# Gates of two blocks for two token groups by Strassen's algorithm, with their input sums and the sums for y moved

## Chip, core and metric

One NeuronCore of a Trainium2 chip. The metric is the device time of one execution in microseconds: the median of three runs, beside the range they cover. PE is the matrix engine, DVE, ACT and POOL (GpSimd) the three others that compute, SP issues most DMAs; POOL issues the accumulating ones.

## What is computed

Banded attention, then two gated feed-forward stages on the 1536 x 512 matrix that it gives, all in float32 with weights stored as float64 words:

```python
scores = scale * q @ k.T + bias + band mask           # 8 global keys, 96 local ones
x = softmax(scores) @ v                               # (2, 8, 768, 64) -> 1536 tokens x 512
a = x @ w1                                            # 512 x 1024
b = x @ w2
h = a * b @ w3                                        # 1024 x 1024
x = h @ w_out                                         # 1024 x 512
out = ((x @ w_a) * (x @ w_b)) @ w_out2                # 512 x 1536, 1536 x 512
```

## The kernel before

Every float32 product is made of three matmuls on split operands (upper part times lower part both ways, and upper times upper), so a matrix is held as a pair hi, lo. The upper part is an ACT copy, the lower part a DVE subtraction (`split`, L742 to L745).

The 1536 tokens are three groups of `TG` = 512. The first feed-forward stage has 8 blocks f of 128 columns of w1 and w2. A **gate** (f, group) makes x @ w1 and x @ w2 for a block and a group: 2 weights x 4 chunks of the 512 inputs x 3 = 24 matmuls of 128x512 (`gate`, L680 to L682); ACT copies the second bank with a sign (L688), and DVE multiplies (L689). A **fold** (f) multiplies w3 of the block with w_out in advance (24 matmuls, `fold`, L244 to L246; ACT stores the result in `wq`, L253). When all gates and folds are there, **y** is the product of `wq` with the gates by a seven-product scheme (`y_product`, 336 matmuls at L942); after it come `products` (1008 matmuls on `ab_band`, again seven products per block) and `output` (`o_band`).

What runs when is written out: `self.order` in `feed_start` lists the gates and folds. Before, it is blocks 0 to 3 group by group, gates of block 4, folds 0 and 1, gates of block 5, folds 2 to 7, gates of blocks 6 and 7, then y. Each engine executes its instructions in the order of the program; `moe` walks the list, and between small steps (`yield`) `feed` emits the next stage of weight conversion: ACT L90, L91, DVE L95, L99, L103, ACT L116, DVE L120 for each piece of weights, loaded by SP into a `raw` buffer. At most six pieces wait.

The operands of y are sums of the gates and of quarters of `wq`. `y_steps` makes them: accumulating DMAs on POOL's queue (L810) write sums in place or into the two buffers `kq01` (free after the attention), and `left` and `right` split them (ACT L822 and L744, DVE L823 and L745). `moe` takes one step behind each gate of blocks 6 and 7, `y_product` the others. The first two raw weights of the second stage (`wab_load`, L747) are loaded and joined in the same steps.

A PSUM bank comes from a pool of eight (`bank`). A matmul that starts a new result in a bank waits until the last reader of that bank is done.

## Time and profile before

| | us |
|---|---|
| median of three runs | 599.81 (599.22 to 599.85) |
| the profiled run | 600.89 |
| its span, first to last instruction | 599.1 |
| PE busy | 584.1 (97%) |
| DVE busy | 442.7 (74%) |
| ACT busy | 366.4 (61%) |
| POOL busy | 168.0 (28%) |

The profile is of one execution, whose own time stands beside its span: what lies around the span is 1.8 us. A busy PE here is a row of overlapping matmuls: each is shown with its whole length, longer than the distance to the next one. "Idle before" is the time in which an engine had nothing to run, with what released it. The gates of block 6 begin at 233.90 us and y at 266.5 us.

### The profile page before, as it was taken

To read this page: it belongs to the slowest core of one execution; us is meant where nothing else is said; L and a number is where in the kernel's file an instruction comes from. 1 tells how busy PE (TensorE), PEld (TensorE's weight loads), DVE (VectorE), ACT (ScalarE), POOL (GpSimd) and SP (SyncE) were. 2 spreads that over 40 slices of the span, in tenths; PEclk is the share of its full clock that TensorE was granted. 3 is DMA by queue.
4 is the path that set the end of the run, shared out by engine and by line. 5 is a ranking of instruction groups with operands and counts; after the bars stand their busy time and mean duration, and the time that the engine had idled before them with its cause. 6 is when DMAs were issued, how large, how long until landed. Compare 5 with 4: busy or idle time off the path is not lost.

```text
span 599.1 us, 10254 instructions
## 1 busy us (share of the span) xinstructions
PE 584.1 (97%) x3632; PEld 509.0 (85%) x3632; DVE 442.7 (74%) x942; ACT 366.4 (61%) x802; POOL 168.0 (28%) x226
## 2 busy tenths in 40 slices
PE   6999999999999999999999999999999999999996
PEld 4678997888888888888899888888888888889996
DVE  5897889539967483649999777777777789984781
ACT  5998889847746473648764544444444465895830
POOL 5653765600000000421612022222222221555500
PEclk9999999999999999999999999999999999999999
DMA  8999683326424332796724112122220248999931
GB/s 228 274 248 236 164 222 106 112 70 212 141 71 141 109 102 70 136 231 126 109 33 139 33 50 79 55 70 71 71 71 2 71 133 220 234 146 193 197 95 57
DMA packets 31821, 76.78 MB, mean 128 GB/s; under 512 B 3601, under 2 KB 11281, under 8 KB 31761
## 3 DMA queue, kind: packets, MB, share of 16 engines
q1 hardware_dynamic: 20560, 57.42, 32.4%
q0 software_dynamic: 10624, 17.83, 18.0%
q10 hardware_dynamic: 576, 0.79, 0.5%
q8 instruction: 30, 0.49, 0.4%
q14 instruction: 31, 0.25, 0.1%
HBM read 55.05 MB, written 3.15 MB: 97 GB/s over the span
## 4 chain that ended last, share of the span: by engine, by line
PE 85%; DMA 9%; DVE 2%; SPq 1%; issue 1%; ACT 0%; POOL 0%; DVEq 0%
PE ab_band L942 29%; PE o_band L942 16%; PE y_band L942 10%; PE ab_band L680 6%; PE ab_band L681 6%; PE ab_band L682 6%; DMA kd_band<-in_kq_dram 3%; PE wfp_band L244 2%; PE wfp_band L246 2%; PE wfp_band L245 2%; DMA v_band<-in_v_dram 2%; PE pv_band L527 2%; DMA kq_band<-in_kq_dram 2%; PE pt_band L491 1%; DMA raw_band<-in_moe_w_dram 1%; DMA qd_band<-in_kq_dram 1%
## 5 line engine op out<-in xcount | busy, mean ns | idle before, releaser
L942 PE MATMUL ab_band<-y_band,ws_band 128*128 128x512 f32 (+1 forms) x576 | 110.1, 337 | 0.0
L942 PEld LDWEIGHTS ab_band<-y_band,ws_band 128*128 128x128 f32 x576 | 91.0, 190 | 12.0
L680 PE MATMUL ab_band<-xh_band,w_band 128*128 128x512 f32 (+1 forms) x216 | 81.8, 379 | 0.0
L682 PE MATMUL ab_band<-xh_band,w_band 128*128 128x512 f32 (+1 forms) x216 | 79.0, 366 | 0.0
L681 PE MATMUL ab_band<-xl_band,w_band 128*128 128x512 f32 (+1 forms) x216 | 79.0, 366 | 0.0
L480 POOL TENSOR_SCALAR s_band<-s_band,z_band 128x256 f32<-128x256 f32 (+1 forms) x96 | 58.3, 622 | 38.8 <-DVE z_band L476 17.8
L942 PE MATMUL o_band<-wo_band,gs_band 128*128 128x256 f32 (+1 forms) x360 | 59.1, 326 | 0.0
L942 PE MATMUL y_band<-gs_band,wf_band 128*128 128x512 f32 (+1 forms) x336 | 58.4, 336 | 0.0
L942 PEld LDWEIGHTS o_band<-wo_band,gs_band 128*128 128x128 f32 x360 | 53.0, 190 | 5.9
L942 PEld LDWEIGHTS y_band<-gs_band,wf_band 128*128 128x128 f32 x336 | 51.8, 190 | 6.6
L942 PE MATMUL ab_band<-y_band,wa_band 128*128 128x512 f32 (+1 forms) x288 | 56.4, 338 | 0.0
L91 ACT ACTIVATE raw_band<-raw_band 128x512 int32<-128x512 uint32 x76 | 51.2, 673 | 0.0
L942 PEld LDWEIGHTS ab_band<-y_band,wa_band 128*128 128x128 f32 x288 | 46.0, 190 | 6.1
L689 DVE TENSOR_TENSOR g_band<-ab_band,b_band 128x512 f32<-128x512 f32 (+1 forms) x27 | 16.9, 628 | 45.2 <-ACT b_band L688 45.2
L463 ACT ACTIVATE s_band<-s_band,m_band 128x256 f32<-128x256 f32 (+1 forms) x96 | 46.7, 493 | 3.2 <-DVE m_band L445 3.2
L680 PEld LDWEIGHTS ab_band<-xh_band,w_band 128*128 128x128 f32 x216 | 40.7, 188 | 7.6 <-issue 1.2
L682 PEld LDWEIGHTS ab_band<-xh_band,w_band 128*128 128x128 f32 x216 | 40.6, 188 | 6.7
L681 PEld LDWEIGHTS ab_band<-xl_band,w_band 128*128 128x128 f32 x216 | 40.7, 189 | 6.1
L1144 ACT COPY p_band<-ab_band 128x512 f32<-128x512 f32 (+1 forms) x48 | 22.0, 481 | 33.4 <-PE ab_band L942 33.2
L810 POOL DMA_DIRECT2D wq_band<-wq_band x4 | 4.6, 1157 | 124.7 <-DVE wf_band L823 123.4
L1145 DVE TENSOR_TENSOR u_band<-ab_band,u_band 128x512 f32<-128x512 f32 (+1 forms) x24 | 13.3, 554 | 33.1 <-PE ab_band L942 32.7
L445 DVE CUSTOM_DVE_ANT_0 s_band<-sp_band,bias_band 128x256 f32<-128x256 f32 (+1 forms) x96 | 37.1, 389 | 0.5 <-ACT bias_band L310 0.4
(160 smaller groups left out, 1258.1 us busy)
## 6 DMA issues: line engine op xcount, KB each, us to landing
raw_band<-in_moe_w_dram SPq DMA_DIRECT2D x31, 512.0 KB, 4.6
raw_band<-in_moe_w_out_dram SPq DMA_DIRECT2D x20, 512.0 KB, 4.4
raw_band<-in_moe_w_b_dram SPq DMA_DIRECT2D x12, 512.0 KB, 3.5
raw_band<-in_moe_w_a_dram SPq DMA_DIRECT2D x12, 512.0 KB, 4.3
ga_band<-ga_band POOLq DMA_DIRECT2D x24, 256.0 KB, 6.7
v_band<-in_v_dram SPq DMA_DIRECT2D x12, 256.0 KB, 8.3
kd_band<-in_kq_dram SPq DMA_DIRECT2D x12, 256.0 KB, 7.8
qd_band<-in_kq_dram SPq DMA_DIRECT2D x12, 256.0 KB, 8.3
```

The lines of the kernel that those rows point to most:

```text
L91: nc.scalar.activation(out=low, in_=low.bitcast(U32), func=AF.Copy, scale=2.0**-29)
L244: nc.tensor.matmul(acc, w[:, 1, k % 4, :], o[:, 0, 0, :], start=(k == 0), stop=False)
L445: nc.vector.tensor_tensor_reduce(out=s[:, j, lo:], in0=sp[:, j, lo:], in1=bias[:, 2 * c + j, :], scale=-self.scale, scalar=FLT_MAX, op0=AL ...
L463: nc.scalar.activation(out=s[:, j, lo:], in_=s[:, j, lo:], func=AF.Exp, bias=m[:, j : j + 1], scale=-1.0, accum_out=z[:, j : j + 1],)
L480: nc.gpsimd.tensor_scalar(out=s[:, j, lo:], in0=s[:, j, lo:], scalar1=z[:, j : j + 1], scalar2=1.0, op0=ALU.mult, op1=ALU.mult)
L680: nc.tensor.matmul(p, wl, xh, start=(c == 0), stop=False)
L681: nc.tensor.matmul(p, wh, xl, start=False, stop=False)
L682: nc.tensor.matmul(p, wh, xh, start=False, stop=(c == self.C - 1))
L689: nc.vector.tensor_tensor(out=out[:, at], in0=ps[0], in1=b, op=ALU.mult)
L942: self.nc.tensor.matmul(bank, wt, xt, start=start and i == n == 0, stop=stop and n == 2 and i == len(terms) - 1, skip_group_check=more,)
L1144: copy = lambda out: nc.scalar.copy(out=out, in_=bank)
L1145: plus = lambda t: nc.vector.tensor_tensor(out=t, in0=bank, in1=t, op=ALU.add)
```

## The change

Gates of blocks 5 and 6 for groups 0 and 1 are made together, as a product of a 2 x 2 matrix of weight quarters (w1 and w2, each cut into two halves of the inputs) with a 2 x 2 matrix of x (two groups, two halves of the inputs). The function `pair` makes seven products of 6 matmuls (2 chunks x 3) where there were eight of 6, in the order 1, 7, 6, 4, 5, 2, 3. Three banks serve a block: the results of products 1, 6, 5 and 3 add up in one of them, and what stands there in between is copied by ACT (behind 1, 7 and 6), added by DVE (behind 4, 5 and 2) or multiplied by DVE (behind 2 and 3).

It needs sums of x and of weights. `x_sums` makes four sums of x in the stretch of the gates of group 2 and block 4 and in the folds, by ACT copies, three POOL additions of 128x1024 (into the second `kq01` buffer) and nine accumulating DMAs on POOL; `x_parts` splits them in fold 7 and in the third gate of block 6. `w_sums` makes the weight sums with four POOL subtractions of 128x256 for each block, and two splits. For these blocks the conversion keeps the joined weights (`g`) and stores them with the opposite sign.

In the order of the program the two pairs stand behind all folds and the third gate of block 6; block 5's gates of groups 0 and 1 have left their place ahead of the folds, so folds 2 to 7 come 48 matmuls sooner. Block 7's gates of groups 0 and 1 are made by `two_gates`, weight by weight; its raw weights are loaded into the two `kq01` buffers when the splits of the sums have read them. The first weights of the second stage are loaded in folds 6 and 7. The steps of `y_steps` are cut smaller and put in another order; eleven of them now lie before y: at three products of the pairs and at eight of the places that `ready` numbers in block 7's gates. In fold, gate and y the matmuls are the same.

PE, the stretch behind the last fold. Before, it is the gate of block 6 for group 0: twelve matmuls of the first weight into one bank, then twelve of the second into the next:

```order
L680 MATMUL ab_band_2967<-xh_band_462,w_band_2851 128x512
L681 MATMUL ab_band_2967<-xl_band_463,w_band_2851 128x512
L682 MATMUL ab_band_2967<-xh_band_462,w_band_2851 128x512
L680 MATMUL ab_band_2980<-xh_band_460,w_band_2864 128x512
L681 MATMUL ab_band_2980<-xl_band_461,w_band_2864 128x512
L682 MATMUL ab_band_2980<-xh_band_460,w_band_2864 128x512
```

Now, in pair 5, six matmuls of product 1 end, product 7 follows in a second bank (`th` are the split sums of x, `ws` those of the weights), and product 6 goes into the first bank again:

```order
L1172 MATMUL ab_band_2987<-xh_band_460,w_band_2397 128x512
L1172 MATMUL ab_band_3000<-th_band_2946,ws_band_2904 128x512
L1172 MATMUL ab_band_3000<-th_band_2947,ws_band_2904 128x512
L1172 MATMUL ab_band_3000<-th_band_2946,ws_band_2904 128x512 x2
L1172 MATMUL ab_band_3000<-th_band_2947,ws_band_2904 128x512
L1172 MATMUL ab_band_3000<-th_band_2946,ws_band_2904 128x512
L1172 MATMUL ab_band_2987<-th_band_2962,ws_band_2904 128x512
L1172 MATMUL ab_band_2987<-th_band_2963,ws_band_2904 128x512
```

The bank `ab_band_2987` is taken up again one product after the one that filled it ended.

ACT in the same stretch. Before, between the first gate of block 6 and the third it copies one bank for each gate (`b_band`), with splits for y and the joining of the second stage's first weights between them:

```order
L688 ACTIVATE b_band_2993<-ab_band_2980 128x512
L822 ACTIVATE wf_band_2996<-wq_band_2530 128x1024
L744 CAST gs_band_3001<-g_band_688 128x1024
L688 ACTIVATE b_band_3037<-ab_band_3024 128x512
L744 CAST gs_band_3040<-g_band_925 128x1024
L865 COPY kq_63<-g_band_2424 128x1024
L822 ACTIVATE wf_band_3047<-wq_band_2530 128x1024
L90 ACTIVATE gb_band_3051<-raw_band_3006 128x512
```

Now the copies of the pairs (`p_band`) stand between the split of the weight sums, the conversion of block 7's first raw weights out of `kq_63`, and the first splits for y:

```order
L804 COPY p_band_2994<-ab_band_2987 128x512
L770 CAST ws_band_2996<-sf_band_2921 128x512
L804 COPY p_band_3007<-ab_band_3000 128x512
L804 COPY p_band_3016<-ab_band_2987 128x512
L770 CAST ws_band_3018<-sf_band_2921 128x512
L92 ACTIVATE g_band_3029<-kq_63 128x512
L93 ACTIVATE kq_63<-kq_63 128x512
L118 CAST w_band_3028<-g_band_3029 128x512
L1061 ACTIVATE wf_band_3059<-wq_band_2549 128x1024
L804 COPY p_band_3072<-ab_band_3065 128x512
L804 COPY p_band_3081<-ab_band_3074 128x512
L984 CAST gs_band_3083<-g_band_688 128x1024
```

The conversion of `kq_63` stands ahead of block 6's first copy, `p_band_3072`.

POOL, the accumulating DMAs for y. Before, the sum of `g_band_925` (gates of group 0, blocks 2 and 3) is made early, and the one that adds it into `kq_64` six places later:

```order
L810 DMA wq_band_2530<-wq_band_2531 128x1024
L810 DMA g_band_688<-g_band_1691 128x1024
L810 DMA g_band_925<-g_band_2053 128x1024
L810 DMA wq_band_2531<-wq_band_2839 128x1024
L810 DMA kq_63<-g_band_688 128x1024
L810 DMA g_band_1691<-g_band_2424 128x1024
L810 DMA wq_band_2530<-wq_band_2839 128x1024
L810 DMA g_band_2373<-kq_63 128x1024
L810 DMA kq_64<-g_band_925 128x1024
```

Now, with nothing between them:

```order
L1050 DMA wq_band_2549<-wq_band_2550 128x1024
L1050 DMA g_band_688<-g_band_1691 128x1024
L1050 DMA wq_band_2550<-wq_band_2800 128x1024
L1050 DMA kq_63<-g_band_688 128x1024
L1050 DMA g_band_1691<-g_band_2440 128x1024
L1050 DMA wq_band_2549<-wq_band_2800 128x1024
L1050 DMA g_band_925<-g_band_2053 128x1024
L1050 DMA kq_64<-g_band_925 128x1024
L1050 DMA g_band_2053<-g_band_3138 128x1024
L1050 DMA g_band_2389<-kq_63 128x1024
```

The DMA into `kq_64` now stands directly behind the one that makes its source, `g_band_925`.

The diff, cut to what the change rests on:

```diff
-        self.order += gates(4) + folds(0, 2) + gates(5) + folds(2, 5) + folds(5, nf)
-        for f in range(6, nf):
-            self.order += gates(f)
+        self.order += gates(4) + folds(0, 2) + gates(5)[2:] + folds(2, nf) + gates(6)[2:]
+        self.order += [("pair", f, 0, whole) for f in self.paired]
+        for f in range(7, nf):
+            self.order += [("two", f, 0, whole), gates(f)[2]]
...
+        self.limit = self.load_limit = len(self.pieces) - 2 * (nf - 1 - self.paired[-1])
...
+            j = self.n_loaded - len(self.pieces)
+            if j >= -2:
+                raw = self.kq01[j].rearrange("p a b c -> p (a b c)").rearrange("p (x y) -> p x y", x=shape[1]).bitcast(I32)
+            else:
+                raw = self.unit("raw", shape, I32)
...
+                if key[0] == "w12" and key[1] in self.paired:
+                    g = self.half("g", [P, a, b])
+                    self.kept.setdefault(key[1], []).append(g)
+                    stages = self.convert(t[:, 0], t[:, 1], raw, g, -1.0)
...
+    def x_sums(self):
+        nc = self.nc
+        add = lambda out, a: nc.gpsimd.dma_start(out, f32(a) if a.dtype == F32R else a, accum_op=ALU.add)
+        (h11, l11), (h21, l21) = self.x[0]
+        (h12, l12), (h22, l22) = self.x[1]
+        t3, t1 = (t.rearrange("p a b c -> p a (b c)") for t in self.kq01)
+        self.sums_x = {3: t3, 1: t1}
+        plus = lambda out, x, y: nc.gpsimd.tensor_tensor(
+            out=out.rearrange("p a b -> p (a b)"), in0=x, in1=y, op=ALU.add
+        )
+        flat = lambda t: f32(t).rearrange("p a b -> p (a b)")
+        nc.scalar.copy(out=t3, in_=f32(h22))
+        yield
+        add(t3, l22)
+        yield
+        t2 = self.sums_x[2] = self.unit("t2", [P, 2, TG])
+        nc.scalar.copy(out=t2, in_=f32(h11))
+        yield
+        plus(t1, flat(h12), flat(l12))
+        add(t3, h12)
+        yield
+        plus(t1, t1.rearrange("p a b -> p (a b)"), flat(h11))
+        add(t2, l11)
+        yield
+        t4 = self.sums_x[4] = [self.half("t4", [P, TG]) for _ in range(2)]
+        for c in range(2):
+            nc.scalar.copy(out=t4[c], in_=f32(h21[:, c]))
+        yield
+        plus(t1, t1.rearrange("p a b -> p (a b)"), flat(l11))
+        add(t3, l12)
+        yield
+        for c in range(2):
+            add(t4[c], l21[:, c])
+        yield
+        yield
+        yield
+        add(t2, t3)
+        yield
+        yield
+        yield
+        yield
+        for c in range(2):
+            add(t4[c], t2[:, c])
+        yield
+    def x_parts(self):
+        self.xt = {}
+        for k in (3, 4, 2, 1):
+            t = self.sums_x.pop(k)
+            hi, lo = ((self.unit if k == 3 else self.late)("th", [P, 2, TG], F32R) for _ in range(2))
+            parts = [(t, slice(None))] if k != 4 else [(t[c], c) for c in range(2)]
+            for src, at in parts:
+                self.nc.scalar.copy(out=hi[:, at], in_=src)
+            yield
+            for src, at in parts:
+                self.nc.vector.tensor_tensor(out=lo[:, at], in0=src, in1=f32(hi[:, at]), op=ALU.subtract)
+            self.xt[k] = hi, lo
+            yield
+    def w_sums(self, f):
+        a, b = self.kept.pop(f)
+        low, high = slice(0, 2), slice(2, 4)
+        if f == self.paired[-1]:
+            st = self.unit("sf", [P, 2, 2, 2, P])
+            s, t = st[:, 0], st[:, 1]
+        else:
+            s, t = (self.half("sf", [P, 2, 2, P]) for _ in range(2))
+        sub = lambda out, x, y: self.nc.gpsimd.tensor_tensor(out=out, in0=x, in1=y, op=ALU.subtract)
+        sub(t[:, 0], b[:, low], b[:, high])
+        sub(s[:, 1], a[:, low], t[:, 0])
+        sub(s[:, 0], b[:, low], a[:, low])
+        sub(t[:, 1], a[:, high], s[:, 1])
+        yield
+        self.ws[f] = []
+        for g in (s, t):
+            w = self.unit("ws", [P, 2, 2, 2, P], F32R)
+            self.ws[f].append(w)
+            self.nc.scalar.copy(out=w[:, 0], in_=g)
+            yield
+            self.nc.vector.tensor_tensor(out=w[:, 1], in0=g, in1=f32(w[:, 0]), op=ALU.subtract)
+            yield
+    def late_parts(self):
+        x, (v, w), o = self.x_parts(), self.w_parts, iter(())
+        for part in (v, v, w, v, v, x, x, x, x, x, x, x, x, o, o, o, w, o, w, o, w, o, w, o):
+            next(part, None)
+            yield
+    def pair(self, f, w, gu, extra):
+        nc = self.nc
+        a, b = w
+        s, t = self.ws.pop(f)
+        part = lambda t, *at: [(t[(slice(None), 0, *at, c)], t[(slice(None), 1, *at, c)]) for c in range(2)]
+        whole = lambda t, cs: [(t[:, 0, c], t[:, 1, c]) for c in cs]
+        left = {
+            1: whole(a, (0, 1)), 2: whole(a, (2, 3)), 4: whole(b, (2, 3)),
+            7: part(s, 0), 6: part(s, 1), 5: part(t, 0), 3: part(t, 1),
+        }
+        right = {1: self.x[0][0], 2: self.x[0][1], 3: self.x[1][1], 7: 3, 6: 2, 4: 4, 5: 1}
+        banks, kept = {}, {}
+        for k in (1, 7, 6, 4, 5, 2, 3):
+            if k in (1, 7, 2):
+                bank = banks[k] = self.bank("ab")
+            bank = banks[{4: 7, 7: 7, 2: 2}.get(k, 1)]
+            hi, lo = self.xt[right[k]] if k > 3 else right[k]
+            self.multiply(bank, left[k], [(hi[:, c], lo[:, c]) for c in range(2)], k in (1, 7, 2), True, k in (6, 4, 5, 3))
+            if k in (1, 7, 6):
+                kept[k] = self.half("p", [P, TG])
+                nc.scalar.copy(out=kept[k], in_=bank)
+            elif k == 3:
+                if f // 2 not in gu[1]:
+                    gu[1][f // 2] = self.late("g1", [P, 2, TG])
+                nc.vector.tensor_tensor(out=gu[1][f // 2][:, f % 2], in0=bank, in1=kept[7], op=ALU.mult)
+            else:
+                t = kept[{4: 6, 5: 7, 2: 1}[k]]
+                nc.vector.tensor_tensor(out=t, in0=bank, in1=t, op=ALU.add)
+                if k == 2:
+                    if f // 2 not in gu[0]:
+                        gu[0][f // 2] = self.late("g1", [P, 2, TG])
+                    nc.vector.scalar_tensor_tensor(
+                        out=gu[0][f // 2][:, f % 2], in0=t, scalar=-1.0, in1=kept[6], op0=ALU.mult, op1=ALU.mult
+                    )
+            for _ in range(2):
+                next(extra, None)
+            yield 1.4
...
+    def two_gates(self, pair, xs, outs, signs):
+        nc = self.nc
+        banks = []
+        for n, w in enumerate(pair):
+            for m, x in enumerate(xs):
+                p = self.bank("ab")
+                banks.append(p)
+                for c in range(self.C):
+                    wh, wl, (xh, xl) = w[:, 0, c, :], w[:, 1, c, :], x(c)
+                    nc.tensor.matmul(p, wl, xh, start=(c == 0), stop=False)
+                    nc.tensor.matmul(p, wh, xl, start=False, stop=False)
+                    nc.tensor.matmul(p, wh, xh, start=False, stop=(c == self.C - 1))
+                    if c == 1:
+                        yield 1.3
+                if n:
+                    b = self.half("b", [P, TG])
+                    nc.scalar.mul(b, p, signs[m])
+                    nc.vector.tensor_tensor(out=outs[m], in0=banks[m], in1=b, op=ALU.mult)
+                yield 1.3
...
+        def ready(i):
+            if i in (0, 1, 2, 3, 5, 8, 9, 11):
+                next(prepare)
+            if i == 4:
+                self.wab_load(1)
+                self.joins[1] = self.wab_join(1)
+            if i > 5:
+                for _ in range(2):
+                    next(self.joins[1], None)
...
+            if what == "pair":
+                if prepare is None:
+                    prepare = self.y_steps(gu)
+                for k, turn in enumerate(self.pair(f, pairs.pop(f), gu, extra)):
+                    if (f, k) in ((5, 6), (6, 1), (6, 4)):
+                        next(prepare)
+                    if (f, k) == (self.paired[0], 0):
+                        self.load_limit += 2
+                        self.feed_load(self.load_limit)
+                    if (f, k) in ((self.paired[0], 3), (self.paired[1], 3)):
+                        self.limit += 1
+                    yield turn
+                continue
...
-        left(1, a11, self.late)
+        left(1, a11)
         add(a11, a21)
+        yield
         right(0, 1, 0, b11[0])
         add(b11[0], b12[0])
-        weights(0, 0)
+        add(a21, a22)
+        yield
+        nc.scalar.copy(out=t2[0], in_=b22[0])
+        add(t2[0], b11[0])
+        add(b12[0], b22[0])
+        yield
+        left(7, a11, self.late)
+        add(a11, a22)
         yield
         right(0, 1, 1, b11[1])
         add(b11[1], b12[1])
-        nc.scalar.copy(out=t2[0], in_=b22[0])
-        add(a21, a22)
-        left(7, a11)
-        weights(0, 4)
-        yield
-        add(t2[0], b11[0])
-        add(b12[0], b22[0])
-        add(a11, a22)
+        yield
         right(0, 2, 0, b21[0])
-        weights(0, 5)
+        yield
+        left(2, a12, self.late, -1.0)
         yield
         b21, b22 = ([gu[t][2 + j] for j in range(2)] for t in range(2))
         c11, c12, c21, c22 = ([gu[2][j + e][:, :, at] for j in range(2)] for e in (0, 2) for at in ends)
-        left(2, a12, self.late, -1.0)
-        right(0, 2, 1, b21[1])
-        add(b21[0], t2[0])
-        yield
         nc.scalar.copy(out=t2[1], in_=b22[1])
         add(t2[1], b11[1])
         add(b12[1], b22[1])
+        yield
+        right(0, 2, 1, b21[1])
+        add(b21[0], t2[0])
+        yield
         left(6, a11, self.unit, -1.0)
         add(a12, a11)
         add(b21[1], t2[1])
...
```

## Rows read from the trace of the kernel before

**Rows 1.** The page: busy time of the engines; TensorE's granted clock in 40 slices.
```profile
PE 584.1 (97%) x3632; PEld 509.0 (85%) x3632; DVE 442.7 (74%) x942; ACT 366.4 (61%) x802; POOL 168.0 (28%) x226
...
PEclk9999999999999999999999999999999999999999
```

**Rows 2.** Waits of PE, whole span: line, releaser: us in total, times, longest.
```profile
PE sp_band L411 <- DMA kq<-in_kq_dram: 5.3, 3, 4.7
...
PE sp_band L428 <- DVE m_band L445: 0.5, 1, 0.5
```

**Rows 3.** The chain of waits in order of time: start us, us, what.
```profile
266.70 58.23 PE y_band L942 x336
324.94 175.88 PE ab_band L942 x1008
```

**Rows 4.** By stretch: busy us of PE, PEld, DVE, ACT, POOL; clock; DMA share; GB/s.
```profile
157.00:165.00 8.00, 8.00 (x37) 6.60 (x37) 7.66 (x14) 5.95 (x15) 0.00 (x0) 1.00 0.39 131
233.90:244.00 10.10, 10.10 (x46) 8.38 (x45) 3.05 (x3) 3.14 (x5) 1.23 (x2) 1.00 0.00 1
244.00:255.00 11.00, 11.00 (x51) 9.09 (x50) 7.60 (x10) 7.21 (x11) 5.01 (x6) 1.00 1.02 190
255.00:266.70 11.70, 11.70 (x53) 9.71 (x52) 4.55 (x6) 4.13 (x5) 2.59 (x3) 1.00 1.06 237
```

**Rows 5.** Timeline of PE: start us, us, engine, line, operation, tiles.
```profile
233.90 0.39 PE L680 MATMUL ab_band<-xh_band,w_band 128*128 128x512 f32 x1
...
239.34 0.39 PE L680 MATMUL ab_band<-xh_band,w_band 128*128 128x512 f32 x1
...
266.54 0.84 PE L942 MATMUL y_band<-gs_band,wf_band 128*128 128x512 f32 x3
```

**Rows 6.** Timeline of ACT, then DVE, behind the first gate of block 6.
```profile
239.54 0.60 ACT L688 ACTIVATE b_band<-ab_band 128x512 f32<-128x512 f32 x1 [4.78 <-PE ab_band L682]
...
240.17 0.69 DVE L689 TENSOR_TENSOR g_band<-ab_band,b_band 128x512 f32<-128x512 f32 x1 [9.62 <-ACT b_band L688]
```

**Rows 7.** Tiles kq, 236 to 300 us: duration ns min/median/max; below, us to landing.
```profile
L744 ACT CAST gs_band<-kq x2: 1054/1057/1060, 270.4 to 273.3; 128x1024 fp32r<-128x1024 f32 x2
L745 DVE TENSOR_TENSOR gs_band<-kq,gs_band x2: 1216/1222/1227, 271.5 to 277.0; 128x1024 fp32r<-128x1024 f32 x2
...
DMA to landing us min/median/max: 7.0/8.4/9.5
```

**Rows 8.** Timeline of DVE, then ACT, 160 to 176 us.
```profile
161.58 0.68 DVE L689 TENSOR_TENSOR g_band<-ab_band,b_band 128x512 f32<-128x512 f32 x1
...
174.95 0.69 DVE L689 TENSOR_TENSOR g_band<-ab_band,b_band 128x512 f32<-128x512 f32 x1 [4.10 <-ACT b_band L688]
...
161.70 0.62 ACT L116 CAST w_band<-g_band 128x512 fp32r<-128x512 f32 x1 [1.26 <-DVE g_band L103]
```

**Rows 9.** Groups of POOL by shape, whole span: count | busy us, mean ns.
```profile
L777 POOL TENSOR_TENSOR sf_band<-ga_band,sf_band 128x256 f32<-128x256 f32 x12 | 13.4, 1114 | 0.9
...
L777 POOL TENSOR_TENSOR sf_band<-ga_band,gb_band 128x256 f32<-128x256 f32 x12 | 9.3, 774 | 48.4 <-DVE ga_band L103 48.4
```

**Rows 10.** Timeline of DVE while POOL adds (128x1024 operations).
```profile
299.99 1.64 DVE L745 TENSOR_TENSOR y_band<-u_band,y_band 128x1024 fp32r<-128x1024 f32 x1
301.56 1.75 DVE L955 TENSOR_TENSOR p_band<-u_band,p_band 128x1024 f32<-128x1024 f32 x1
```

**Rows 11.** Tiles raw_band (raw weights), 130 to 300 us: time to landing.
```profile
DMA to landing us min/median/max: 3.4/4.2/12.3
```

**Rows 12.** Timeline of POOL, ACT and DVE around the sums for y.
```profile
242.67 1.03 POOL L810 DMA_DIRECT2D wq_band<-wq_band  x1 [123.43 <-DVE wf_band L823]
...
266.71 1.06 ACT L822 ACTIVATE wf_band<-wq_band 128x1024 fp32r<-128x1024 f32 x1 [3.00 <-DMA wq_band<-wq_band]
...
277.04 1.22 DVE L745 TENSOR_TENSOR gs_band<-kq,gs_band 128x1024 fp32r<-128x1024 f32 x1
```

**Rows 13.** Tiles wq_band, 236 to 300 us: time to landing of the accumulating DMAs.
```profile
DMA to landing us min/median/max: 4.7/9.1/15.0
```

More of the change, by code (lines that the diff above doesn't have):

```diff
@@ L49, in __init__ @@
         self.pairs_from = 16
+        self.paired = (5, 6)
+        self.kept, self.ws = {}, {}
         self.sums = {}
@@ L723, in moe @@
             }[tg]
-            yield from self.gate(pairs[f], xs(tg), gu[tg][q][:, f % 2], at, signs)
-            if n == last[f]:
+            if f == self.paired[-1]:
+                for _ in sums:
+                    pass
+            for turn in self.gate(pairs[f], xs(tg), gu[tg][q][:, f % 2], at, signs):
+                if tg == 2 and 0 < f < 4 or f == 4 and tg:
+                    next(sums, None)
+                if f == self.paired[-1]:
+                    for _ in range(3):
+                        next(extra, None)
+                if f == nf - 1:
+                    ready(early)
+                    early += 1
+                yield turn
+            if f == self.paired[-1]:
+                for _ in range(3):
+                    next(extra, None)
+            if n == last[f] and f not in self.paired:
                 pairs[f] = None
-            if f >= nf - 2:
-                if prepare is None:
-                    prepare = self.y_steps(gu)
-                next(prepare)
+            if f >= nf - 1:
+                ready(early)
+                early += 1
             yield 1.3 * (at.stop - at.start) / TG
@@ L847, in adds @@
                 add(out[j], a[j])
-        def weights(f, n):
-            if f not in joins:
-                self.wab_load(f)
-                joins[f] = self.wab_join(f)
-            for _ in range(n):
-                next(joins[f], None)
-        joins = {}
-        left(1, a11, self.late)
+        left(1, a11)
         add(a11, a21)
+        yield
         right(0, 1, 0, b11[0])
         add(b11[0], b12[0])
-        weights(0, 0)
+        add(a21, a22)
[6 more added lines that the diff above has]
+        add(a11, a22)
         yield
@@ L881, in y_steps @@
         yield
-        nc.scalar.copy(out=t2[1], in_=b22[1])
-        add(t2[1], b11[1])
-        add(b12[1], b22[1])
         left(6, a11, self.unit, -1.0)
@@ L895, in y_steps @@
         right(0, 6, 1, t2[1])
-        weights(1, 3)
         yield
```

58 lines of the change are left out of this document (47 added, 11 removed).

## Prediction

> **What bounds the kernel now.** I read the page's engine summary first, then the waits of PE, the chain of waits, the table by stretch, and last the single rows around the places that the change touches. The summary has PE busy for 97% of the span, at a granted clock that never falls [rows 1]. All of PE's waits together are about 10 us, all at lines of the attention (the longest group 5.3 us, the shortest 0.5 us) [rows 2]. From the y product on the chain of waits is PE alone, in two unbroken pieces that meet without a gap (266.70 + 58.23 = 324.93 against 324.94) [rows 3]. In the stretches shown, from 157 to 165 and from 233.9 to 266.7 us, PE is busy from end to end, while DVE has 15.2 us of work in the last three, 32.8 us [rows 4]. So here a matmul removed is its time gained, as long as everything that PE needs still comes before PE asks for it.
>
> The pace: the gates of blocks 6 and 7 are 144 matmuls of 128x512; the first starts at 233.90, the first of y at 266.54 [rows 5]. 32.64 / 144 = 0.2267 us each. (The 0.39 us in the rows is one matmul's own length; they overlap.)
>
> **The change, term by term.** The sum is made against the profiled run (600.89 us, span 599.1) and put on the median, 599.81, as a difference.
>
> *Removed.* A block's gates for groups 0 and 1 are 2 groups x 2 weights x 4 chunks x 3 = 48 matmuls; the seven products are 7 x 2 chunks x 3 = 42. Two blocks: 12 fewer, 12 x 0.2267 = **2.72 us**, all on PE's path. Nothing else is taken from or given to PE: folds, y, the later products and the output keep their matmuls.
>
> *Added on ACT and DVE.* With 0.60 us for a 128x512 copy and 0.69 for a DVE operation of that size [rows 6], 1.05 and 1.22 us for 128x1024 [rows 7]: ACT gets 3.3 (copies of x) + 4.35 (upper parts of the x sums) + 2.4 (of the weight sums) + 3.6 (six copies per block) - 2.4 (four evacuations gone) = 11.3 us. DVE gets 5.0 + 2.7 + 10 x 0.69 - 2.8 = 11.8 us. Both have that room under PE, so I take nothing for it, unless one operation is late for its place. There are four such places.
>
> 1. *Hand-offs of the banks inside a block.* A product is 6 x 0.2267 = 1.36 us, and in PE's new order the same bank is written again one product after its result was read: four tight hand-offs per block, eight in all. Before, the first matmul behind a gate starts at 239.34, ACT's copy runs 239.54 to 240.14, DVE's operation takes 0.69 [rows 5, 6]. So a copy is over 0.80 us into the next product and a DVE add 0.20 + 0.69 = 0.89: 0.56 and 0.47 us to spare. In ACT's new order only one of these copies (block 6, third product) has a 1.05 us operation right ahead of it, which itself starts early; it keeps about 0.3. Cost taken: 0; bound: the spare times are used up eight times by a 1.05 us operation, 8 x 0.49 = 3.9.
>
> 2. *The x sums, at 142 to 165 us.* Here DVE is nearly full (7.66 of 8.00 us) [rows 4] and behind PE: it reads the second gate of group 2 only at 161.58 and is done by 162.26 [rows 8], while that bank is wanted again 300 matmuls ahead of 233.90, at 165.9: 3.6 us to spare. New there are four ACT copies and three GpSimd adds of 128x1024. ACT's next conversion step waits for DVE anyway (1.26 us idle before it) [rows 8], so a copy in front delays little. A GpSimd add of 128x256 took 0.77 to 1.11 us on the mean [rows 9], so an estimate for 128x1024 is four times that, 3.1 to 4.5 us; the first falls just ahead of that read. Beside such adds DVE's 1.22 us operations took 1.64 and 1.75 us [rows 10], 34 to 43% longer: over 4.5 us that is at most 1.9 us, less than 3.6. Cost taken: 0. After it, DVE has an idle gap of 4.10 us [rows 8] before the folds.
>
> 3. *The x parts and block 7's weights.* Pair 5 starts at T = 233.90 - 48 x 0.2267 + 24 x 0.2267 = 228.46 (block 5's gates for two groups now lie behind the folds, block 6's third ahead). ACT's splits queue behind the last fold's evacuation at T - 5.4; counting 0.4 to 1.05 us each, then 0.7 to 1.22 on DVE, the parts are there at T - 1.9 (third sum, wanted at T + 1.36), T + 0.6 (second, T + 2.72) and T + 1.8 (first, T + 5.44). Smallest spare time 2.1 us. Block 7's raw weights now go into the buffers that these splits free, and ACT's conversion of them stands in its queue ahead of block 6's first copy, due at T + 12.2. A load landed 3.4 to 12.3 us after issue [rows 11]; from T - 1.9 that is T + 1.5 to T + 10.4, and with 4.5 us of conversion behind it a stall of up to 2.7 us at the far end, none below a landing at T + 7.7. The median, 4.2, gives none: cost 0.
>
> 4. *The y sums.* The accumulating DMAs begin at about T + 12.5 (block 5 ends at T + 9.5; its last DVE operation 0.9, a split of 1.22, an issue on POOL of 1.03 us [rows 12]), and y at T + 156 x 0.2267 = T + 35.4 = 263.8. The tight one is the second sum in the kq buffers, wanted 54 matmuls into y, T + 47.6. Before, its DVE split ended 277.04 + 1.22 = 278.26 for a need at 266.54 + 12.24 = 278.78: already only 0.5 us early [rows 12]. Now its DMA stands on POOL's queue right behind the one whose result it adds, so it is not issued before that one has landed. With 190 to 237 GB/s [rows 4], 512 KB take 2.2 to 2.8 us; seven adds and one or two raw loads make 17.6 to 25.2 us, so T + 30.1 to T + 37.7. The next add lands 7.0 to 9.5 us later [rows 7], and ACT and DVE need 1.05 + 1.22: ready at T + 39.4 to T + 49.5. The middle (T + 44.6) is 3 us early; the far end 1.8 us late. Cost taken: 0, since the medians leave room.
>
> Sum: 600.89 - 2.72 = 598.2 for the profiled run, **597.1** for the median.
>
> **A rule against the trace.** The [rows 10] show a slowing of DVE beside GpSimd, not a stop. The Trainium skill, "SBUF — State Buffer", section "SBUF: two separate sides", says that DVE operations with two SBUF inputs and GpSimd operations share a port pair by an exclusive lock, so that the loser waits for the whole instruction. The trace is short of that: adds of 0.77 to 1.11 us beside them [rows 9] cost an operation 0.42 and 0.53 us. What a full stop would do is rival D.
>
> **The rivals.**
>
> A (forecast): all 2.72 us arrive. 597.1. For it: PE's unbroken chain, and spare times at each place. Chance 0.60.
>
> B: the hand-offs stall PE by 0.2 to 0.4 us each, 8 x 0.2 to 0.4 = 1.6 to 3.2 us: 598.7 to 600.3, mostly no change. It needs ACT or DVE to be busy with something else at the instant a product ends; the order shows that once in eight, and both engines are about half idle there. Chance 0.13.
>
> C (slower): the chained y sum. If the second of the two adds lands as late as the slowest add before (15.0 us [rows 13]; ACT waited 3.00 us for such an add [rows 12]), its split is ready at T + 37.7 + 15.0 + 2.3 = T + 55.0, a stall of 7.3 us: 604.4. It gives a slower kernel once the stall is over 2.72 + 1.2 = 3.9 us, a landing after T + 49.3; between 1.5 and 3.9 us it cancels the gain. For it: ACT is in order, so later copies wait behind this one, and DMA is full there. Against: the 15.0 was the last of a burst, while this one is issued when the burst is nearly through. Chance 0.18, of which 0.13 slower.
>
> D: GpSimd's first 128x1024 add stops DVE for all of it: 161.58 + 4.5 + 0.68 = 166.8, 0.9 us after the bank is wanted; the other adds fall into DVE's slack. 598.0, still faster. Chance 0.05, half of it with a further stall to no change.
>
> E: PE was not the bound and nothing changes, 599.8. Against it stand [rows 2, 3]: 0.02. A further 0.02 is left for a late weight in place 3 that undoes the gain.
>
> **How the numbers follow.** A measurement of this kernel tells 0.2%, 1.2 us, from no change, so faster means below 598.6. Faster: A 0.60 + half of D 0.03 = 0.63. Same: B 0.11, C 0.05, D 0.02, E and the late weight 0.04 = 0.22. Slower: C 0.13, B 0.02 = 0.15. The likeliest is A, 597.1. The range goes from 596.5 (the runs before lie 0.6 us apart) up through B and the mild end of C to 600.8; about 0.15 is left above and 0.05 below.
>
> **What would show it.** Right: 12 matmuls fewer in PE's rows, pairs of 9.5 us each, y starting 2.7 us sooner (263.8) and no PE wait between 130 us and the end of y. Wrong: a wait of PE on the banks or on ACT copies inside the pairs (B), on the split of a kq buffer about 12 us into y (C), on a gate's bank at 163 to 169 us (D), or DVE operations lengthened there by more than half. If the stalls at places 1 to 4 add up to over 1.5 us, the forecast of a measurable gain falls.

## The result, and the profile after

| | us |
|---|---|
| before, median of nine runs | 599.85 (599.22 to 600.65) |
| changed, median of nine runs | 606.59 (600.67 to 607.05) |
| ratio | 1.0098, 95% interval 1.0073 to 1.0124 |
| profiled run of the changed kernel | 606.28, span 604.3 |

The change makes the kernel 1% slower. The forecast was 597.1, with a range that ended at 600.8. Eight of the nine runs lie between 605.06 and 607.05; of the ninth, 600.67, there is no trace. The profiled run of the kernel before took 600.89, more than any of its nine, so the two profiles differ by less (5.4 us) than the medians (6.74).

The page of the changed kernel, engine summary and granted clock, against [rows 1]. The 12 matmuls are gone (3632 to 3620), and in one slice the clock falls:

```profile
PE 583.3 (97%) x3620; PEld 507.0 (84%) x3620; DVE 466.0 (77%) x957; ACT 376.1 (62%) x817; POOL 191.6 (32%) x246
...
PEclk9999999999979999999999999999999999999999
```

The waits of PE, against [rows 2]. The attention's are as before. Three are new: one for a DVE operation of a gate, two inside y.

```profile
PE ab_band L830 <- DVE g_band L839: 3.9, 1, 3.9
...
PE y_band L1172 <- ACT u_band L1226: 0.7, 1, 0.7
...
PE y_band L1172 <- ACT p_band L1226: 0.4, 1, 0.4
```

**Where 5.2 us of span came from (604.3 against 599.1).** PE came out of the attention 1.06 us sooner in this execution, and from there to 161.90 us every matmul is ahead by that much. (In the traces of the runs below the same matmuls are 0.02 to 1.63 us ahead, in kernels that are the same up to there or nearly so, so this is not put down to the change.) Fold 0 began at 174.06 us before and begins at 179.96 now, 5.90 us later, so 6.96 us were lost from 161.90 on. y then starts at 269.71 where it was 266.54, so 2.73 us were won back between: the twelve matmuls. y itself lasts 60.16 us where it lasted 58.23: 1.93 lost. 6.96 - 2.73 + 1.93 = 6.16 us lost by the change; less the 1.06 of the attention that is 5.10 of the 5.2.

The pairs are what the forecast said they would be. In the timeline of PE the first matmul of block 5's pair and of block 6's:

```profile
234.35 0.39 PE L1172 MATMUL ab_band<-xh_band,w_band 128*128 128x512 f32 x1
...
243.87 0.39 PE L1172 MATMUL ab_band<-xh_band,w_band 128*128 128x512 f32 x1
```

9.52 us, 42 x 0.2267, with no wait; the second pair takes as long (`two_gates` begins at 253.39). The loss is elsewhere, in two places.

**Place one, 153 to 175 us.** Timeline of PE: the first matmul behind a short hold, the last ahead of the long wait, the first behind it, and the first two that come faster again:

```profile
162.41 0.50 PE L830 MATMUL ab_band<-xh_band,w_band 128*128 128x512 f32 x1
...
165.07 0.39 PE L832 MATMUL ab_band<-xh_band,w_band 128*128 128x512 f32 x1
169.32 0.80 PE L830 MATMUL ab_band<-xh_band,w_band 128*128 128x512 f32 x1 [3.86 <-DVE g_band L839]
...
174.18 0.45 PE L832 MATMUL ab_band<-xh_band,w_band 128*128 128x512 f32 x1
174.48 0.40 PE L830 MATMUL ab_band<-xh_band,w_band 128*128 128x512 f32 x1
```

The matmul at 162.41 needs a bank that ACT copies only at 161.69 to 162.36, late because ACT's conversion step at 158.57 had waited 3.66 us for DVE; by 165.07 PE is 0.44 us behind. From 165.07 to 169.32 PE starts nothing: 4.02 us more than a matmul's distance. The twelve matmuls from 169.32 to 174.48 then take 5.16 us where they took 2.72: 2.44 us. Together 6.90 of the 6.96. The table by stretch shows why the twelve are slow: the columns are as in [rows 4], the clock the one ahead of the DMA share:

```profile
167.00:168.00 1.00, 0.00 (x0) 0.00 (x0) 1.00 (x1) 0.00 (x0) 1.00 (x1) 0.74 1.11 221
...
169.00:174.00 5.00, 4.68 (x11) 3.72 (x12) 4.30 (x8) 4.78 (x11) 2.68 (x3) 0.50 1.03 197
...
175.00:176.00 1.00, 1.00 (x6) 0.83 (x5) 0.86 (x2) 0.41 (x1) 0.00 (x0) 1.00 1.12 193
```

With PE idle, the granted clock goes to 0.50, 1.2 GHz, and comes back to 2.4 GHz only at 174 to 175 us, when PE had been at work again for some five us.

What PE waited for is DVE's evacuation of the second gate of group 2, at 168.59 in place of 161.58 [rows 8]. Timeline of DVE:

```profile
153.65 3.33 DVE L97 TENSOR_SCALAR g_band<-g_band 128x512 int32<-128x512 int32 x1
...
162.01 3.45 DVE L101 SCALAR_TENSOR_TENSOR g_band<-raw_band,g_band 128x512 int32<-128x512 int32 x1
165.60 3.07 DVE L105 CUSTOM_DVE_ANT_0 g_band<-raw_band,g_band 128x1024 uint16<-128x1024 uint16 x1
168.59 0.68 DVE L839 TENSOR_TENSOR g_band<-ab_band,b_band 128x512 f32<-128x512 f32 x1
```

The operation at L97 takes 0.42 us alone (as at 161.55, in the same timeline); here 3.33. L101 and L105 take 0.69 alone; here 3.45 and 3.07. Timeline of POOL at the same time:

```profile
153.97 2.71 POOL L699 TENSOR_TENSOR kq<-xh_band,xl_band 128x1024 f32<-128x1024 f32 x1
...
162.20 2.70 POOL L699 TENSOR_TENSOR kq<-kq,xh_band 128x1024 f32<-128x1024 f32 x1
...
165.15 2.96 POOL L699 TENSOR_TENSOR kq<-kq,xl_band 128x1024 f32<-128x1024 f32 x1
```

Each long DVE operation stands beside one of the three GpSimd additions and ends just behind it: additions end at 156.68, 164.90 and 168.11 (start and length added), the operations at 156.98, 165.46 and 168.67. DVE was not slowed, it stood still until GpSimd had finished. It lost 2.91 + 2.76 + 2.38 = 8.05 us. 3.6 of them were to spare, PE itself came 0.44 late, and the rest, 4.0, is PE's wait.

**Place two, y.** Timeline of PE, the rows of y with a wait (0.44 and 0.71 us):

```profile
314.14 8.89 PE L1172 MATMUL y_band<-gs_band,wf_band 128*128 128x256 f32 x72 [0.44 <-ACT p_band L1226]
323.75 6.28 PE L1172 MATMUL y_band<-gs_band,wf_band 128*128 128x256 f32 x48 [0.71 <-ACT u_band L1226]
```

ACT and DVE have no work for over 5 us in the early part of y, which they then lack later. Timelines of POOL, ACT and DVE there, against [rows 12]:

```profile
258.55 0.86 POOL L1050 DMA_DIRECT2D g_band<-g_band  x1 [0.27 <-DVE gs_band L985]
272.03 0.86 POOL L1050 DMA_DIRECT2D kq<-g_band  x1 [12.62 <-ACT gs_band L984]
...
273.63 1.91 POOL L1050 DMA_DIRECT2D wq_band<-wq_band  x1
```

```profile
276.76 1.05 ACT L984 CAST gs_band<-kq 128x1024 fp32r<-128x1024 f32 x1 [3.35 <-DMA kq<-g_band]
...
285.32 3.05 ACT L984 CAST gs_band<-g_band 128x1024 fp32r<-128x1024 f32 x4 [5.59 <-issue]
```

```profile
279.76 1.23 DVE L985 TENSOR_TENSOR gs_band<-g_band,gs_band 128x1024 fp32r<-128x1024 f32 x1 [0.69 <-ACT gs_band L984]
286.40 2.43 DVE L985 TENSOR_TENSOR gs_band<-g_band,gs_band 128x1024 fp32r<-128x1024 f32 x3 [5.41 <-ACT gs_band L984]
```

The add into `g_band`, issued at 258.55, makes the source of the next DMA on POOL's queue. That one goes out at 272.03, after a wait of 12.62 us, and three more stand behind it. The row names ACT as the releaser; in the program this DMA waits for the landing of the other, which took 12.9 us, to 271.45, the longest of the DMAs that read or write `g_band` there:

```profile
DMA to landing us min/median/max: 4.7/8.7/12.9
```

The last of the three, the sum of two quarters of `wq` (273.63), landed 11.6 us after its issue, at 285.23. ACT's next split starts at 285.32 and DVE's at 286.40, after 5.41 us idle. ACT's row names no releaser ("issue"), but the same row of a run below, the one with the sum by DMA, names this DMA:

```profile
279.20 3.04 ACT L985 CAST gs_band<-g_band 128x1024 fp32r<-128x1024 f32 x4 [5.64 <-DMA wq_band<-wq_band]
```

That split reads gates, not this sum, so by the program it can only be waiting for memory that the DMA still uses; no run tests this. A run without this DMA, below, has no such gap.

The delay lasts to the place where PE feels it: ACT's copy of `p_band`, for which the matmuls at 314.14 wait, starts 44.0 us into y, where it started 41.6 us into y before. PE's two waits are 1.15 of the 1.93 us that y lost.

### The profile page after: what moved, and what is told of

It reads as the page before. It is cut to its first block, busy times and chain, and to the rows that moved or that the text cites. A ratio compares the mean times of both kernels' runs of the same rounds, so it can differ in the third digit from the quotient of the medians.

```text
span 604.3 us, 10314 instructions
## 1 busy us (share of the span) xinstructions
PE 583.3 (97%) x3620; PEld 507.0 (84%) x3620; DVE 466.0 (77%) x957; ACT 376.1 (62%) x817; POOL 191.6 (32%) x246
## 4 chain that ended last, share of the span: by engine, by line
PE 68%; DMA 11%; DVE 11%; issue 4%; ACT 3%; SPq 1%; POOL 1%; DVEq 0%; POOLq 0%; ACTq 0%
PE ab_band L1172 32%; PE o_band L1172 15%; DMA kd_band<-in_kq_dram 3%; PE ab_band L830 3%; DMA v_band<-in_v_dram 2%; PE ab_band L831 2%; PE ab_band L832 2%; PE wfp_band L264 2%; PE wfp_band L263 2%; PE wfp_band L262 2%; DMA g_band<-g_band 2%; DVE gs_band L985 2%; PE pv_band L545 2%; DMA kq_band<-in_kq_dram 2%; PE pt_band L509 2%
## 5 line engine op out<-in xcount | busy, mean ns | idle before, releaser
L498 POOL TENSOR_SCALAR s_band<-s_band,z_band 128x256 f32<-128x256 f32 (+1 forms) x96 | 56.9, 608 | 37.5 <-DVE z_band L494 18.0
L830 PE MATMUL ab_band<-xh_band,w_band 128*128 128x512 f32 (+1 forms) x168 | 64.4, 383 | 4.0 <-DVE g_band L839 3.9
L831 PE MATMUL ab_band<-xl_band,w_band 128*128 128x512 f32 (+1 forms) x168 | 61.3, 365 | 0.0
L832 PE MATMUL ab_band<-xh_band,w_band 128*128 128x512 f32 (+1 forms) x168 | 61.1, 364 | 0.0
L93 ACT ACTIVATE raw_band<-raw_band 128x512 int32<-128x512 uint32 x74 | 49.6, 670 | 0.0
L830 PEld LDWEIGHTS ab_band<-xh_band,w_band 128*128 128x128 f32 x168 | 32.2, 192 | 10.8 <-DVE g_band L839 4.3
L1017 POOL TENSOR_TENSOR sf_band<-gb_band 128x256 f32<-128x256 f32 x12 | 10.3, 862 | 94.2 <-DVE gb_band L105 75.2
L118 ACT CAST w_band<-g_band 128x512 fp32r<-128x512 f32 x36 | 22.5, 624 | 25.9 <-DVE g_band L105 25.7
L832 PEld LDWEIGHTS ab_band<-xh_band,w_band 128*128 128x128 f32 x168 | 32.2, 192 | 5.1
L831 PEld LDWEIGHTS ab_band<-xl_band,w_band 128*128 128x128 f32 x168 | 32.3, 192 | 4.4
```

What stands on the lines that cost most here:

```text
L93: nc.scalar.activation(out=low, in_=low.bitcast(U32), func=AF.Copy, scale=2.0**-29)
L118: nc.scalar.mul(hi, g, sign) if sign < 0 else nc.scalar.copy(out=hi, in_=g)
L498: nc.gpsimd.tensor_scalar(out=s[:, j, lo:], in0=s[:, j, lo:], scalar1=z[:, j : j + 1], scalar2=1.0, op0=ALU.mult, op1=ALU.mult)
L830: nc.tensor.matmul(p, wl, xh, start=(c == 0), stop=False)
L831: nc.tensor.matmul(p, wh, xl, start=False, stop=False)
L832: nc.tensor.matmul(p, wh, xh, start=False, stop=(c == self.C - 1))
```

## Experiments

Theory G: a GpSimd addition holds DVE for as long as it runs; the bank comes late; PE waits and its clock falls. Rival R: the copies and DMAs of the x sums delay the weight conversion. For y, theory Y1: sums that land late hold ACT and DVE; rival Y2: DVE has simply too much to do there.

**Without the three additions.**

```diff
-        plus(t1, flat(h12), flat(l12))
...
-        plus(t1, t1.rearrange("p a b -> p (a b)"), flat(h11))
...
-        plus(t1, t1.rearrange("p a b -> p (a b)"), flat(l11))
```

> The changed kernel without the three GpSimd additions of 128x1024 among the x sums; the fourth x sum then holds what lies in its buffer, so that part of the computation is left out. Theory G (a GpSimd addition holds DVE for the length of the whole instruction, the gate's bank comes late, PE waits and its granted clock falls): PE's 3.9 us wait at 165 to 169 us and the stretch at the lower clock are gone, about 6.7 us less than the changed kernel, 598.3 to 599.5 (the forecast 597.1 and the 1.2 us of waits in y). Rival R (ACT's four copies and the accumulating DMAs of the x sums delay the weight conversion): they are all still there, so 605 to 607.

Measured: 599.26, ratio to before 0.9990 (0.9979 to 1.0001). No wait of PE between the attention and y; in y 0.7 and 0.6 us. R falls: all its copies and DMAs are still there, and in its trace PE loses nothing between the attention and fold 0.

**The same sum by DMA.**

```diff
-        plus(t1, flat(h12), flat(l12))
+        nc.scalar.copy(out=t1, in_=f32(h12))
...
+        add(t1, l12)
...
+        add(t1, h11)
...
+        add(t1, l11)
```

The other two `plus` lines are taken out.

> The changed kernel with the same sum made by one more ACT copy of 128x1024 and three more accumulating DMAs, in place of the three GpSimd additions. Theory G: no long DVE instruction between 150 and 170 us, no PE wait there, 598 to 600. Rival R: more copies and more DMA, so as late as the changed kernel or later, 606 to 609.

Measured: 599.96, ratio 0.9988 (0.9976 to 1.0000). One more ACT copy and three more DMAs of 512 KB cost nothing that shows; the additions on GpSimd did.

**The additions cut into quarters.**

```diff
...
+            for i in range(4):
+                at = slice(i * TG // 2, (i + 1) * TG // 2)
+                nc.gpsimd.tensor_tensor(out=o[:, at], in0=x[:, at], in1=y[:, at], op=ALU.add)
```

> The changed kernel with each of the three GpSimd additions cut into four of 128x256: the same work on GpSimd, some 8.4 us, in 12 instructions. Theory G with a hold for a whole instruction: no DVE instruction is longer than its own time plus about 0.8 us, and DVE and GpSimd take turns, so that DVE loses less in all, 3 to 6 us where it lost 8, and PE waits 0 to 2 us: 598.5 to 603. If the two engines shared the port by bandwidth, DVE would lose the same 8 us and the time stay at 605 to 607.

Measured: 608.69, ratio 1.0140 (1.0122 to 1.0158), slower still; the expectation fails. Timelines of POOL and of DVE:

```profile
154.85 3.13 POOL L703 TENSOR_TENSOR kq<-xh_band,xl_band 128x256 f32<-128x256 f32 x4
...
162.89 3.09 POOL L703 TENSOR_TENSOR kq<-kq,xh_band 128x256 f32<-128x256 f32 x4
```

```profile
154.54 3.73 DVE L97 TENSOR_SCALAR g_band<-g_band 128x512 int32<-128x512 int32 x1
...
162.84 3.93 DVE L97 TENSOR_SCALAR g_band<-g_band 128x512 int32<-128x512 int32 x1
```

POOL's rows hold four additions each (x4). DVE gets no turn between them: one DVE operation of 0.42 us lasts 3.73 us, through all four. So here it counts how long GpSimd adds without a break, not how long one instruction is.

**The additions alone, in the kernel before.**

```diff
+                if tg == 2 and 0 < f < 4:
+                    next(sums, None)
```

`sums` is a generator that makes the three GpSimd additions into a kq buffer, one after the other.

> The kernel before with nothing but the three GpSimd additions put in at the same place of the program (into a kq buffer that is not read before it is written again). Theory G: DVE loses about 8 us at 152 to 168 us, the bank of the second gate of group 2 is some 4 us late, PE's clock falls, 604 to 607. Rival R: three additions on an engine that is idle cost nothing, 599.9.

Measured: 599.84, ratio 0.9997 (0.9987 to 1.0007): no loss, against the expectation. But the additions did not run where they were written. Nothing on POOL's queue held them, and they ran 35 us sooner, under the attention. Timeline of POOL, and the DVE operation that ran beside the second of them:

```profile
118.28 2.39 POOL L698 TENSOR_TENSOR kq<-xh_band,xl_band 128x1024 f32<-128x1024 f32 x1
120.75 2.38 POOL L698 TENSOR_TENSOR kq<-kq,xh_band 128x1024 f32<-128x1024 f32 x1
```

```profile
122.40 0.69 DVE L689 TENSOR_TENSOR g_band<-ab_band,b_band 128x512 f32<-128x512 f32 x1 [3.04 <-ACT b_band L688]
```

Alone an addition takes 2.4 us. And this DVE operation, which reads a PSUM bank and one SBUF tile, has its usual 0.69 us: not every DVE operation is held. (Two subtractions of the attention beside the first addition, and two beside the third, read PSUM and SBUF too; they are not held either: 0.76 us for each two, 0.42 for a single one at 111.99.) The experiment as I meant it needed the copy and the DMAs in front, which hold POOL's queue:

**The additions held back, in the kernel before.**

```diff
+        nc.scalar.copy(out=t3, in_=f32(h22))
...
+        add(t3, l22)
...
+        plus(flat(h12), flat(l12))
+        add(t3, h12)
...
+        plus(out, flat(h11))
...
+        plus(out, flat(l11))
```

> The kernel before with the start of the x sums alone: ACT's copy of 128x1024 into the first kq buffer, the two accumulating DMAs into it, and the three GpSimd additions behind them, which so run at 152 to 168 us as in the changed kernel (nothing reads the sums). Theory G: DVE loses about 8 us there, PE waits 3 to 4.5 us for the bank of a gate of block 4 and then runs some 7 us at the lower clock: 604 to 607. Rival (the pairs or the folds in a new order are what costs): 599.9, as in the run whose three additions had run ahead, under the attention.

Measured: 606.99 (four runs, 603.7 to 608.85), ratio 1.0094 (1.0057 to 1.0131). Nothing else of the change is in this kernel, and it loses 6.5 us. POOL, DVE and PE's wait:

```profile
154.93 2.73 POOL L700 TENSOR_TENSOR kq<-xh_band,xl_band 128x1024 f32<-128x1024 f32 x1
...
160.78 2.69 POOL L700 TENSOR_TENSOR kq<-kq,xh_band 128x1024 f32<-128x1024 f32 x1
```

```profile
154.62 3.33 DVE L95 TENSOR_SCALAR g_band<-g_band 128x512 int32<-128x512 int32 x1
...
160.48 3.56 DVE L99 SCALAR_TENSOR_TENSOR g_band<-raw_band,g_band 128x512 int32<-128x512 int32 x1
164.17 2.61 DVE L103 CUSTOM_DVE_ANT_0 g_band<-raw_band,g_band 128x1024 uint16<-128x1024 uint16 x1
```

```profile
PE ab_band L680 <- ACT b_band L688: 4.8, 1, 4.8
```

The bank that PE waits for is here one that ACT frees (the one that cost the changed kernel 0.44 us): ACT's step ahead of that copy had waited 5.58 us for DVE's held conversion. So the hold reaches PE by either engine.

**The additions later, in the folds.**

```diff
-        plus(t1, flat(h12), flat(l12))
...
         for c in range(2):
             add(t4[c], t2[:, c])
...
+        plus(t1, flat(h12), flat(l12))
...
```

The other two additions move likewise.

> The changed kernel with the three GpSimd additions of 128x1024 put behind the accumulating DMAs of the x sums on POOL's queue, so that they run in the first folds, some 25 us later. Theory G says that a GpSimd addition holds DVE whenever it runs: DVE instructions of about 3 us must appear beside them there too, but no gate waits for a bank behind them, so the 3.9 us wait of PE at 165 us and the lower clock behind it are gone: 598 to 601, near the kernel with DMA additions (599.96). If the loss were the additions themselves and not their place, 605 to 607.

Measured: 600.54, ratio 1.0006 (0.9996 to 1.0015). POOL and DVE:

```profile
181.87 3.04 POOL L699 TENSOR_TENSOR kq<-xh_band,xl_band 128x1024 f32<-128x1024 f32 x1
184.99 2.75 POOL L699 TENSOR_TENSOR kq<-kq,xh_band 128x1024 f32<-128x1024 f32 x1
```

```profile
181.81 3.67 DVE L105 CUSTOM_DVE_ANT_0 g_band<-raw_band,g_band 128x1024 uint16<-128x1024 uint16 x1
185.40 2.63 DVE L97 TENSOR_SCALAR g_band<-g_band 128x512 int32<-128x512 int32 x1
```

DVE is held there nearly as long (3.67, 2.63 and 2.77 us, 7.3 us lost), but PE waits for nothing of it at the time. Later it does, a little: 0.7 us for a copy in a pair and 0.2 for a split of an x sum. The gain is still not there; the waits in y (0.7 and 0.5) are.

**The additions on DVE itself.**

```diff
-        plus = lambda out, x, y: nc.gpsimd.tensor_tensor(
+        plus = lambda out, x, y: nc.vector.tensor_tensor(
```

> The changed kernel with the three additions of 128x1024 on DVE itself. There they take 1.22 us each, 3.7 us in all, less than the 8 us that DVE lost to them on GpSimd, and in DVE's order they stand behind the multiplication that frees the bank. Theory G: no PE wait at 165 us; the waits in y remain: 599 to 600.5. If an addition in this stretch costs the same wherever it runs, 605 to 607.

Measured: 598.78, ratio 0.9982 (0.9971 to 0.9993), 0.2 us below the range expected; of PE's waits in y one is left, 0.7 us. DVE, with the evacuation that PE needs ahead of the first of them:

```profile
160.11 0.68 DVE L839 TENSOR_TENSOR g_band<-ab_band,b_band 128x512 f32<-128x512 f32 x1
...
161.31 1.22 DVE L699 TENSOR_TENSOR kq<-xh_band,xl_band 128x1024 f32<-128x1024 f32 x1
```

3.7 us of DVE in place of 8.05.

**Without one sum of `wq` quarters.** The base is the kernel with DMA additions.

```diff
-        add(a12, a11)
```

> The kernel with DMA additions without the one accumulating DMA that adds one quarter of the folded weights to another for the sixth product of y's left operand (so that part of the computation is left out). ACT's wait of 5.6 us at about 279 us for that DMA is gone. Theory Y1: DVE's idle gap behind it (5.5 us) goes too, and with it PE's two waits in y: 0.8 to 1.5 us under the kernel with DMA additions, 598.4 to 599.2. Theory Y2: 599.9 as there.

Measured: 597.67, ratio 0.9951 (0.9933 to 0.9969). PE has no wait in y, and the gaps of over 5 us on ACT and DVE are gone, though POOL's queue is held as long as in the changed kernel (12.75 us). One DMA less, on an engine that PE never waits for directly, is worth 2.3 us against the base (599.96): Y1, by more than the 0.8 to 1.5 expected. The expectation counted PE's listed waits; the loss is that y lasts 60.05 us in the base and 58.23 here. This edit also takes 512 KB from the DMA queues; the next run keeps that DMA.

**The y sums sooner.** The same base.

```diff
-                    if (f, k) in ((5, 6), (6, 1), (6, 4)):
+                    if (f, k) in ((5, 1), (5, 4), (6, 1)):
```

> The kernel with DMA additions and the first three steps of the y sums taken at the second and fifth product of block 5's pair and at the second of block 6's, instead of the last of block 5 and the second and fifth of block 6: about 5 us sooner. Theory Y1 (PE's two waits in y, 1.05 us together, come from sums that land late, and hold ACT and DVE behind them): the waits shrink to under 0.4 us and the time falls by 0.7 to 1.5 us against the 599.96 of the kernel with DMA additions, 598.4 to 599.2. Theory Y2 (DVE simply has too much to do in y): no change, 599.9.

Measured: 597.64, ratio 0.9951 (0.9932 to 0.9970): faster than the kernel before and than the changed one, with the whole computation in it, and again by more than Y1 expected (598.4 to 599.2). Timeline of PE, y and the first row behind it:

```profile
263.80 58.40 PE L1173 MATMUL y_band<-gs_band,wf_band 128*128 128x512 f32 x336
322.03 1.55 PE L1173 MATMUL ab_band<-y_band,wa_band 128*128 128x512 f32 x6
```

58.23 us again, without a gap, as before [rows 3], and y starts 2.74 us sooner than it did [rows 5]. The gain, 2.87 us of the median beside it (600.51), is the 2.72 of the forecast.

**Both together: GpSimd additions, y sums sooner.**

```diff
-                    if (f, k) in ((5, 6), (6, 1), (6, 4)):
+                    if (f, k) in ((5, 1), (5, 4), (6, 1)):
```

> The changed kernel with its GpSimd additions and the earlier steps of the y sums (second and fifth product of block 5's pair, second of block 6's). If the two losses are separate, PE's wait at 165 us and the lower clock stay and only the waits in y go: some 1.2 to 2.3 us under the changed kernel, 604.3 to 605.4. If the late y sums were a consequence of the late gate, no more than 0.5 us.

Measured: 603.92, ratio 1.0050 (1.0025 to 1.0074), 2.7 us under the changed kernel, a little more than the 1.2 to 2.3 expected. PE's wait for the gate is as it was, and y is whole:

```profile
PE ab_band L830 <- DVE g_band L839: 3.8, 1, 3.8
```

```profile
269.67 58.40 PE L1172 MATMUL y_band<-gs_band,wf_band 128*128 128x512 f32 x336
327.90 1.55 PE L1172 MATMUL ab_band<-y_band,wa_band 128*128 128x512 f32 x6
```

The two losses are separate. Of this kernel's ten runs two lie at 598.48 and 599.74; as with the ninth run of the changed kernel, there is no trace of them.

## Why the prediction was wrong, point by point

**The bound and the matmuls: right.** PE is the bound, 12 matmuls are 2.72 us, and all of it arrives once the two losses are taken out (597.64; forecast 597.1).

**Hand-offs inside the pairs (place 1): right.** Two pairs of 9.52 us without a wait. Rival B did not happen.

**The x sums (place 2): the step that failed.** It put DVE's slowing beside GpSimd at 34 to 43%, from two operations of 1.64 and 1.75 us [rows 10], and so at 1.9 us at most against 3.6 to spare. DVE lost 8.05. The rows were read as a rate, and they are a wait. POOL's rows beside them, from the timeline of the kernel before:

```profile
299.41 1.13 POOL L777 TENSOR_TENSOR sf_band<-sf_band,ga_band 128x256 f32<-128x256 f32 x1
300.62 1.61 POOL L777 TENSOR_TENSOR sf_band<-ga_band,sf_band 128x256 f32<-128x256 f32 x1
```

The first ends at 300.54. DVE's operation began at 299.99, so it had 0.55 us of that addition left to wait for, and was 0.42 late. The second ends at 302.23; DVE's began at 301.56, had 0.67 us left, and was 0.53 late. An operation that comes at the end of a hold pays only what is left of it. The starts and ends of both engines would have told this; the lengths alone do not. Second, the step counted one addition of the three against the bank. The first was over at 156.68; the second and third ran back to back, right ahead of the evacuation, and cost 2.76 and 2.38 us. (The length of an addition, estimated at 3.1 to 4.5 us, was 2.70 to 2.96.)

**The clock: not in the sum.** The forecast priced a late bank at its lateness. The wait of 4.02 us cost 2.44 more, because PE ran at 1.2 GHz for the 5 us behind it.

**The rule that spoke against the change was right.** Rival D, with a chance of 0.05, was the mechanism; its price of 0.9 us was wrong, since it charged one addition and no clock. Its sign, a wait on a gate's bank at 163 to 169 us, is what came. The Trainium skill, "SBUF — State Buffer", section "SBUF: two separate sides", states an exclusive lock that is held for the whole instruction; the 3.33 us of an operation that needs 0.42 agree with it. The same section lists, on DVE's side, operations with two SBUF inputs and ones in a two-port mode: the held L97 has one SBUF input, and whether it runs in that mode no row shows; the operation that ran freely reads PSUM and SBUF. I weighed the rule against two rows that agree with it, and took them for evidence against.

**Block 7's weights (place 3): right.** No wait there.

**The y sums (place 4): the price of the tight one was right, but another one cost.** The second kq sum was split by 277.84 + 1.23 = 279.07, 9.36 us into y; it was wanted at 12.24, so 2.9 us early, where the middle of the estimate said 3. But the step stopped at the tightest sum. The DMA that holds POOL's queue for it (12.62 us) delays the three behind it as well, and the last of these left ACT and DVE without work for over 5 us. PE felt that only 28 us later, at 314 us, when ACT, behind a DVE that was full again, was 2.4 us late; it cost 1.93 us. Rival C's remark that ACT is in order, so that what stands behind a late sum waits as well, was the mechanism; the place it named was not.

## To carry to other kernels

Work put on GpSimd is not free because GpSimd is idle: while it adds in SBUF, the DVE operations on SBUF beside it stood still in these traces, and three additions cost DVE 8 us that would have cost 3.7 on DVE itself. If it must be there, put it where DVE has room until the next thing that PE needs, and check by starts and ends, not by lengths, whether two engines hold each other up. On an in-order queue count what stands behind a waiting DMA too: idle time that it opens on a nearly full engine is paid later, where nothing points back to it.

## What the runs showed of the hardware that was not expected

- Four GpSimd additions of 128x256 in a row hold a DVE operation as one of 128x1024 does: 3.73 us through all four. DVE gets no turn between them.
- A DVE operation with an input in PSUM had its usual 0.69 us beside a GpSimd addition; one with a single SBUF input and an SBUF output was held for 2.9 us.
- The rows do not tell who is held by who begins first: the row of the held L97 begins at 153.65, 0.32 us ahead of the addition's, and L101's at 162.01, 0.19 ahead.
- A wait of PE of 4.02 us was followed by 5 us of work at 1.2 GHz, which cost another 2.44 us. In the traces of the additions in quarters, of the additions held back and of the last experiment, waits of 5.1, 5.0 and 4.0 us cost another 2.7, 3.0 and 1.8.
- Still open: why single runs of kernels with this loss come out at 598.5 to 600.7 us. A hold that falls on a DVE operation that PE does not need could do it; no such run was traced.
